# Strassen weight sums in another order: rounding of weights ahead of a batch's squares, GpSimd's staged sums regrouped, one chunk's last sums on VectorE

## The chip, the cores and the metric

The kernel runs on one core of a Trainium2 chip. The time is device microseconds of one execution; three executions of the kernel before gave 928.67, 924.08 and 924.61 us, median 924.61 us. A core has TensorE (PE, matrix products), VectorE (DVE), ScalarE (ACT), GpSimd (POOL) and SyncE (SP, which only issues DMAs here). Each engine works through its own list of instructions in order.

## The reference

Two blocks follow one another. Attention without a softmax: for each of 8 batches and 8 heads, with 576 positions and 64 channels, in float32,

```
kv  = einsum('bhsd,bhse->bhde', k, v)
out = einsum('bhsd,bhde->bhse', q, kv)
x   = out / sqrt(mean(out*out, axis=-1) + 1e-6) * g_norm     # then as (4608, 512)
h   = x @ w_in                    # (4608, 512) @ (512, 2048)
y   = maximum(0.01*h, h) @ w_out  # (4608, 2048) @ (2048, 512)
```

The two weight matrices arrive as float64 and have to be rounded to float32 on the chip; `x`, `h` and `y` are float32.

## The kernel before, in words

The 4608 rows of `x` are nine blocks of 512. The 2048 columns of `h` are four *chunks* `c` of 2 x 256 columns each. A product of two 2x2 block matrices is done in Strassen's way, with seven products in place of eight; the order of the seven is `ORDER = (1, 2, 6, 5, 7, 3, 4)`. Each needs sums of blocks of its sides, and those sums are what VectorE and GpSimd spend much of their time on.

**First block** (`first_block`, L1121; about 40 to 115 us). Block 0 of `x` meets chunks 0 to 2 without Strassen, while the weights are still coming. Step n of 12 does the product `h_ps` (n), a leaky ReLU on ScalarE (L1139), and the product `o_acc` of step n-1. In between, `between(n, half)` (L1168) works through the table `plan` (L1160): a number is a weight tile ("job") whose rounding is started with `round_w`, `f` finishes all roundings begun, `t` is a step of batch 0's attention tail, `a` one of the 14 steps of batch 1's attention (7 and 8 are its squares and copies out of PSUM, L415 and L421; 9 to 14 its division by the root mean square), `x` the four VectorE sums of block 1's Strassen sides. A rounding is two ScalarE instructions (L264 `add`, L262 `cut`), one on VectorE (L266), one on ScalarE (L271) and two on VectorE (L281, L284). Everything here but the sums of `x` keeps its written order on each engine. Starting a rounding also issues loads of later tiles: seven raw places (three in `stage`, four in `pairs`) hold jobs 0 to 23, then the two halves of `early` and the first third of `stage` serve jobs 24 on. Job 21 is the `w_in` tile of step 11; jobs 19, 17 those of steps 10, 9; jobs 22 and 23 are `w_out` tiles of steps 10 and 11; jobs 24 to 27 belong to chunk 3's `w_out` and are not needed for another hundred microseconds.

**Block 1 and the rest of block 0** (`rounds`, L1233; about 115 to 235 us). Now one-level Strassen runs on block 1 with chunks 0 to 3 and then on block 0 with chunk 3. Each chunk is seven *slots* t; the number of a slot over all chunks is `at = 7 * now + t`. A slot does one of the seven `h` products and, from slot 9 on, one of the seven `o` products of the chunk before. GpSimd makes, in this written order and with no freedom to reorder: `sides_w1(c)` (L702: sums of `w_in` for products 5 and 6, into the first quarter of `pairs`), its second part `more` (products 7 and 3, second quarter), `sides_w2` sums (L738), the `gs` sums of the activations (L916), and `combine(c, part)` (L780). GpSimd's first instruction of this stage (L1193) is a copy of one element that waits for the last of block 1's `x` sums.

`combine` prepares what comes after: from block 2 on the `h` products use Strassen twice, and the second-level sums of `w_in` are the same for all blocks, so they are made once, staged in `stage`, and written by SP to `w1_dram`. Part 0 uses products 5 and 6's sides, part 1 those of 7 and 3, part 2 the weights themselves (products 1, 2 together, then 4 alone). Parts 0 and 1 are four sums of 128x256 each; part 2 is four of 128x256 and four of 128x128. A sum's place in `stage` is the next third in the cycle 1, 2, 0. `put_off` hands the DMA to SP some slots later.

**Blocks 2 to 8** (about 235 to 925 us). Two-level Strassen; `read` (L814) brings the seven-fold weights from `w1_dram` into a ring of five places laid over the first-level weights. `sides_x(i)` makes `x`'s sums, its `inner` (L861) the second-level ones on GpSimd into `stage`.

Of the kernel before, what the change touches and what calls it, by code (L numbers as in the profile page):

```python
# [24 lines left out]
def kernel(  # L25
# [36 lines left out]
    nc = tc.nc  # L62
    B, H, S, D = q.shape
    DM, DF = w_in.shape
    P = 128
# [41 lines left out]
    NW = U * NE * P  # L107
# [589 lines left out]
    def add(eng, out_, a, b_, minus=False, pinned=False):  # L697
        ins = eng.tensor_tensor(out_, a, b_, op=ALU.subtract if minus else ALU.add)  # L698
        if pinned or steady or in_block_1:
            pin(ins)  # L700
# [74 lines left out]
    NG = 7 * P  # L775
    SLOT = {1: 0, 2: 1, 4: 2, 5: 3, 6: 4, 7: 5, 3: 6}
    w1_dram = [dram.tile([P, 7, 7, P], F32, name=f"w1_{c}") for c in range(NC)]
    stage_homes = itertools.cycle([view(stage, i * NW, NW) for i in (1, 2, 0)])

    def combine(c, part):  # L780


        direct = w1_sb[0][c].rearrange("p u (t r) m -> p u r t m", t=2)
        last = w1_sb[1][c][:, :, 2:, :].unsqueeze(3)
        parts = [((5, 6), pair(0, U, 2, 2, P))], [((7, 3), pair(1, U, 2, 2, P))], \
            [((1, 2), direct), ((4,), last)]

        for js, y in parts[part]:
            t = view(next(stage_homes), 0, 4, len(js), P)
            s1, s2, s3, s4 = (t[:, i, :, :] for i in range(4))  # L790
            y11, y12, y21, y22 = (y[:, u, r, :, :] for u in range(2) for r in range(2))

            add(nc.gpsimd, s1, y21, y22)
            add(nc.gpsimd, s2, s1, y11, True)
            add(nc.gpsimd, s3, y11, y21, True)
            add(nc.gpsimd, s4, y12, s2, True)
            to = w1_dram[c][:, :, AT[js[0]]:AT[js[0]] + len(js), :]
            if js[0] == 1:
                for r in range(2):
                    put_off(to[:, r, :, :], y[:, 0, r, :, :], 2 - part // 2)  # L800
            else:
                put_off(to[:, :2, :, :], y[:, 0, :, :, :], 2 - part // 2)
            put_off(to[:, 2, :, :], y22, 2 - part // 2)
            put_off(to[:, 3:, :, :], t, 2 - part // 2)


    reads = [(c, k) for _ in range(2, NB) for c in range(NC) for k in ORDER]
# [313 lines left out]
    def first_block(between):  # L1121
# [27 lines left out]
        for t in range(4):  # L1149
# [10 lines left out]
    plan = {(1, 0): (5, f, t), (1, 1): (t, 6, f, t), (2, 0): (t, 7, f, t), (2, 1): (8, f, t, t),  # L1160
            (3, 0): (9, f, t, a), (3, 1): (10, f), (4, 0): (11, f, a), (4, 1): (12, f),
            (5, 0): (13, f, a), (5, 1): (14, f), (6, 0): (15, f), (6, 1): (16, f),
            (7, 0): (a, a, 17, f), (7, 1): (a, 18, f), (8, 0): (a, 19, 24, f),
            (8, 1): (a, 20, 25, f), (9, 0): (a, a, 21, f), (9, 1): (a, 22, a, f),
            (10, 0): (a, 23, f, a), (10, 1): (x,), (11, 0): (26, f)}
    loaded, x_sides = 12, None

    def between(n, half):  # L1168
        nonlocal loaded, x_sides
        for what in plan.get((n, half), ()):  # L1170
            if what == f:
                finish_w()
            elif what == x:
                x_sides, _, sums, _ = sides_x(1)
                go(sums)
            elif what in (t, a):
                go(tail if what == t else a_steps, 1)
            else:
                round_w(what)
                to = what + 7 if what < 17 else {22: 28, 23: 28, 26: 28}.get(what, 25)  # L1180
                while loaded <= min(to, 31):
                    load_w(loaded)
                    loaded += 1
                    if loaded in (13, 16):
                        load_pair(1, {13: 2, 16: 3}[loaded], homes=homes_1[{13: 2, 16: 3}[loaded]])
# [8 lines left out]
    h_sides, more = sides_w1(0)  # L1194
    more()
    sides_w2(0)[1](0)
    for part in range(2):
        combine(0, part)
    sides_w2(0)[1](1)
    in_loop = True  # L1200

    LATE_ONE = {15: 2, 16: 2, 17: 1, 18: 1, 19: 2}
    A_SLOTS = {18: 1, 19: 2, 22: 1, 23: 1, 24: 2, 25: 1, 26: 1, 27: 2, 28: 1, 29: 1, 30: 1, 31: 1,
               34: 2}
    DIRECT = {23: 0, 25: 1, 27: 2, 29: 3}
    READS = {28: 2, 30: 4, 32: RING}
    PARTS = {33: ("11", "12"), 35: ("22",), 37: ("21",)}

    FINE_SLOTS = {1: 1, 2: 1, 4: 1, 9: 1, 10: 2, 11: 1, 12: 1, 15: 1, 16: 2, 17: 2, 18: 1, 19: 1,
# [24 lines left out]
    for i, chunks in rounds:  # L1234
# [7 lines left out]
        for c in chunks:  # L1242
            now += 1
            nxt = units[now + 1] if now + 1 < len(units) else (NB, 0)
            g_sides = {}
            h_steps = product_h(now, h_sides, x_sides, g_sides) if one else \
                product_h_two(i, c, now, quarters, g_sides, second_of(now - 2))
            for t in range(7):
                slot = 7 * c + t
                go(h_steps, 1)  # L1250
                if not one:

                    if t == 6:
                        go(h_steps, 1)
                    if slot in LATE_SLOTS:
                        go(late, 1)
                    for _ in range(FINE_SLOTS.get(slot, 0)):
                        go(a_steps, 1)
                    if i + 1 < NB:
                        if slot == 20:  # L1260
                            x_sides, new_quarters, sums, inner = sides_x(i + 1)
                        if slot in (20, 21, 22):
                            go(sums, 2 if slot == 20 else 1)
                        if slot == 24:
                            inner(0)
                        elif slot == 25:
                            inner(1)
                    load_some()

                if now - 1 in seconds:  # L1270
                    for half in range(2):
                        if t == (6 if half else 4):
                            inner_g(now - 1, half)
                    if t == 5 and now - 1 < 2 * NC + NC - K:
                        inner_w2(units[now - 1][1])
                if (7 * now + t == 7 * NC + 4):
                    while writes:
                        pin(nc.sync.dma_start(*writes.pop()))
                if slot in HELD and i == NB - 1:
                    pass  # L1280
                elif waited == LAG:
                    go_o()
                elif o_queue:
                    waited += 1
                write_later()
                at = 7 * now + t
                for key in PARTS.get(at, ()):
                    if at == 33:
                        part_os = os
                    load_part(part_os, key)  # L1290
                if at in READS:
                    read(READS[at])
                if one:
                    if at in DIRECT:
                        combine(DIRECT[at], 2)
                    if t == 3 and nxt[0] < 2 and nxt[1] != c:
                        h_sides, more_h = sides_w1(nxt[1])
                        combine(nxt[1], 0)
                    if t == 5 and nxt[0] < 2 and nxt[1] != c:
                        more_h()  # L1300
                    if t == 0 and units[now - 1][1] != c and now > 0:
                        combine(c, 1)
                    if not rest and rounded < len(w_jobs):
                        steps = rounding(rounded)
                        rest.extend((3, 3, 1))
                        rounded += 1
                    if rest:
                        go(steps, rest.popleft())
                    if loaded < min(rounded + 2, len(w_jobs)):
                        load_w(loaded)  # L1310
                        loaded += 1
                    if at in (15, 16):
                        load_pair(2, at - 15)
                    go(late, LATE_ONE.get(at, 0))
                    go(a_steps, A_SLOTS.get(at, 0))
                    load_some(2 if at in (19, 20) else 1)
                    if at == 7 * NC - 4:
                        x_sides, _, sums, _ = sides_x(0)
                    elif at == 7 * N1 - 4:
                        x_sides, new_quarters, sums, inner = sides_x(2)  # L1320
                    if at in (7 * NC - 4, 7 * NC - 3, 7 * N1 - 4, 7 * N1 - 3):
                        go(sums, 2)
                    if at == 7 * N1 - 3:
                        inner(0)
                    elif at == 7 * N1 - 2:
                        inner(1)

            for _ in range(2 if i == NB - 1 and c == NC - 1 else 0):
                go(h_steps, 1)
                go_o()  # L1330
            go(h_steps)
            if c == NC - 1 and i != 1 and i + 1 < NB:
                inner(2)
                quarters = new_quarters
            by_two = NC + NC - K <= now < len(units) - 2
            if by_two:
                seconds[now] = (os, store(i))
            o_queue.append(product_o(now, g_sides, os, store(i), by_two))
# [32 lines left out]
```

## Time and profile before

| what | us |
|---|---|
| median of three executions | 924.61 |
| the profiled execution, its own time | 926.94 |
| its span, first to last instruction | 925.1 |
| TensorE busy in it (matmul) | 909.7 |
| GpSimd busy | 392.9 |
| VectorE busy | 610.7 |
| ScalarE busy | 347.6 |

The profiled execution was 2.33 us above the median, and 1.84 us of its time lie outside its span. "Busy" of TensorE counts a product that runs at half clock like any other. Where a row has `[4.78 <-POOL pairs L698]` the engine stood idle 4.78 us ahead of it, until an instruction of GpSimd that writes `pairs` was done. L698 is the helper `add`, so nearly all sums of VectorE and GpSimd carry that line and are told apart by the tiles they name.

### The profile page before, as it was taken

How to read it: one execution, taken by the hardware profiler on the slowest of the kernel's cores; microseconds unless marked ns; L12 is line 12 of the kernel's file. 1: busy time of each engine (PE TensorE's matmuls, PEld its weight loads, DVE VectorE, ACT ScalarE, POOL GpSimd, SP SyncE). 2: the span in 40 equal slices, each digit the busy share in tenths (PEclk: the TensorE clock that was granted, in tenths of full speed). 3: DMA queues.
4: the chain of work that ended last, by engine and by line, in shares of the span. 5: the costliest groups of instructions: out<-in, count | busy, mean ns of one | idle time of the engine just before them, and what ended most of it. 6: DMA issues, size and time to landing. Idle time of an engine off the chain costs nothing.

```text
span 925.1 us, 18145 instructions
## 1 busy us (share of the span) xinstructions
PE 909.7 (98%) x7024; PEld 786.1 (85%) x7024; DVE 610.7 (66%) x1119; ACT 347.6 (38%) x679; POOL 392.9 (42%) x475
## 2 busy tenths in 40 slices
PE   8999979999999999999999999999999999999998
PEld 4444468888898999999999999999999999999997
DVE  5764863556556877577856785687658755755565
ACT  5756543222334332433243324333343333223330
POOL 2000099988642374216422642264225522543322
PEclk9999999999999999999999999999999999999999
DMA  9997264897999678867897788757765676667632
GB/s 262 244 243 200 68 226 153 256 279 226 287 310 309 218 224 250 260 218 219 246 268 231 223 232 263 236 165 219 241 179 181 187 220 200 183 188 221 199 116 92
DMA packets 92405, 202.16 MB, mean 219 GB/s; under 512 B 10016, under 2 KB 44448, under 8 KB 92320
## 3 DMA queue, kind: packets, MB, share of 16 engines
q1 hardware_dynamic: 81344, 189.14, 69.0%
q10 hardware_dynamic: 10528, 10.69, 3.4%
q8 instruction: 56, 0.92, 0.4%
q0 software_dynamic: 448, 1.18, 0.3%
q14 instruction: 29, 0.24, 0.1%
HBM read 173.44 MB, written 27.53 MB: 217 GB/s over the span
## 4 chain that ended last, share of the span: by engine, by line
PE 84%; DMA 9%; POOL 2%; DVE 2%; issue 1%; ACT 1%; SPq 0%; POOLq 0%; ACTq 0%; DVEq 0%
PE o_c L126 19%; PE o_a L126 18%; PE h_ha L126 11%; PE h_hb L126 10%; PE h_hc L126 8%; PE h_hd L126 8%; DMA stage<-in_moe_w_in_dram 3%; PE o_ps L126 2%; DMA pairs<-in_moe_w_in_dram 2%; DMA q_in<-in_q_dram 2%; PE h_b L126 2%; PE h_a L126 2%; POOL pairs L698 1%; PE h_c L126 1%; POOL stage L698 1%
## 5 line engine op out<-in xcount | busy, mean ns | idle before, releaser
L698 POOL TENSOR_TENSOR gs<-g 128x512 f32<-128x512 f32 x66 | 84.0, 1272 | 249.5 <-ACT g L909 249.5
L909 ACT ACTIVATE g<-g 128x512 f32<-128x512 f32 x127 | 80.1, 631 | 142.5 <-DVE g L698 142.5
L1028 ACT COPY w_all<-h_ha 128x512 f32<-128x512 f32 x84 | 49.0, 583 | 171.0 <-PE h_ha L126 165.3
L126 PE MATMUL o_c<-pairs,gs 128*128 128x256 f32 x392 | 93.2, 381 | 0.0
L126 PE MATMUL o_a<-pairs,gs 128*128 128x256 f32 x392 | 93.0, 380 | 0.0
L698 DVE TENSOR_TENSOR o<-h_hb,o 128x128 f32<-128x128 f32 x104 | 29.9, 287 | 83.2 <-ACT pairs L1028 83.1
L698 DVE TENSOR_TENSOR o<-o_a,o 128x512 f32<-128x512 f32 (+1 forms) x93 | 62.7, 674 | 30.4 <-PE o_a L126 30.1
L126 PEld LDWEIGHTS o_c<-pairs,gs 128*128 128x128 f32 x392 | 71.3, 190 | 9.4 <-POOL pairs L698 1.2
L126 PEld LDWEIGHTS o_a<-pairs,gs 128*128 128x128 f32 x392 | 71.3, 190 | 8.1
L698 DVE TENSOR_TENSOR o<-o_c,o 128x512 f32<-128x512 f32 x80 | 54.8, 686 | 31.8 <-PE o_c L126 31.7
L126 PE MATMUL h_ha<-stage,w_all 128*128 128x128 f32 x448 | 59.9, 276 | 1.4 <-POOL stage L698 1.4
L126 PEld LDWEIGHTS h_ha<-stage,w_all 128*128 128x128 f32 x448 | 56.7, 192 | 4.6 <-POOL stage L698 1.6
L698 DVE TENSOR_TENSOR g<-g,pairs 128x512 f32<-128x512 f32 x84 | 55.7, 689 | 1.9
L698 POOL TENSOR_TENSOR pairs<-g 128x128 f32<-128x128 f32 x52 | 23.8, 457 | 75.7 <-PE h_hb L126 47.4
L698 DVE TENSOR_TENSOR w_all<-h_hc,w_all 128x512 f32<-128x512 f32 x56 | 38.4, 685 | 15.8 <-PE h_hc L126 15.5
L698 DVE TENSOR_TENSOR o<-h_hd,o 128x128 f32<-128x128 f32 x78 | 22.2, 284 | 38.2 <-ACT pairs L1028 38.0
L126 PE MATMUL h_ps<-xT,w_all 128*128 128x512 f32 (+1 forms) x104 | 45.0, 580 | 2.0 <-DVE w_all L284 2.0
L126 PE MATMUL h_hb<-stage,w_all 128*128 128x128 f32 x336 | 46.7, 275 | 0.0
L1193 POOL COPY pairs<-xt 1x1 f32<-1x1 f32 x1 | 0.2, 177 | 108.0 <-PE o_acc L126 108.0
L1028 ACT COPY pairs<-h_hb 128x384 f32<-128x384 f32 x84 | 40.1, 477 | 13.8 <-PE h_hb L126 12.9
L698 POOL TENSOR_TENSOR gs<-g,gs 128x512 f32<-128x512 f32 x33 | 45.2, 1369 | 0.0
L698 POOL TENSOR_TENSOR gs<-gs,g 128x512 f32<-128x512 f32 x33 | 44.1, 1335 | 2.6
(237 smaller groups left out, 2280.5 us busy)
## 6 DMA issues: line engine op xcount, KB each, us to landing
w_all<-w SPq DMA_DIRECT2D x196, 448.0 KB, 4.1
pairs<-w SPq DMA_DIRECT2D x56, 512.0 KB, 4.3
out_dram<-o ACTq DMA_DIRECT2D x35, 256.0 KB, 5.1
v_in<-in_v_dram SPq DMA_DIRECT2D x27, 288.0 KB, 4.7
k_in<-in_k_dram SPq DMA_DIRECT2D x26, 288.0 KB, 4.4
q_in<-in_q_dram SPq DMA_DIRECT2D x52, 144.0 KB, 5.6
q_in<-in_q_dram SPq DMA_DIRECT2D x52, 140.0 KB, 5.5
w<-stage SPq DMA_DIRECT2D x12, 512.0 KB, 4.2
```

Source lines behind the costliest of these rows:

```text
L126: pin(nc.tensor.matmul(*args, **kw))
L698: ins = eng.tensor_tensor(out_, a, b_, op=ALU.subtract if minus else ALU.add)
L909: first_turn(nc.scalar.activation(t, t if src is None else src, func=AF.Prelu, alpha=SLOPE))
L1028: nc.scalar.copy(q[:, at], bank)
L1193: pin(nc.gpsimd.tensor_copy(pair(0, NW)[:1, :1], x_sides[4][:1, 0, :1]))
```

## The change

Three things change; the work computed is the same.

1. `plan`: jobs 19 to 25 are rounded in the order of their numbers, where before it was 19, 24, 20, 25, 21, 22, 23, and 19 to 22 one at a time with `f` after each. Jobs 20 and 21 stand between attention steps 7 and 8, job 23 ahead of steps 9 and 10. Which loads a rounding triggers follows: job 26's load goes with job 21, 27's with 24, 28's with 25.
2. GpSimd's order: `combine` becomes a generator with a pause after each two sums. Ahead of the loop only `combine(0, 0)` is made; `combine(0, 1)` follows `sides_w1(1)` in slot 3; `combine(c, 0)` and `combine(c, 1)` for c from 1 to 3 stand together in slot t = 0 of chunk c. `combine(0, 2)` moves from GpSimd in slot 23 to VectorE in slots 15, 16, 18 and 19, two sums each. The last parts of chunks 1, 2, 3 move from slots 25, 27, 29 to 24, 26, 28.
3. `HOMES` names each staged sum's place in `stage`, in units of 512 columns; the sources that exist already are handed to SP a slot or two sooner, and reads from `w1_dram` begin in slot 22 in place of 28 and end their first five in slot 30 in place of 32.

```diff
-    stage_homes = itertools.cycle([view(stage, i * NW, NW) for i in (1, 2, 0)])
-    def combine(c, part):
+    HOMES = {(0, 0): (2,), (0, 1): (4,), (1, 0): (0,), (1, 1): (2,), (2, 0): (4,), (2, 1): (0,),
+             (3, 0): (4,), (3, 1): (0,), (0, 2): (2, 4), (1, 2): (2, 4), (2, 2): (0, 2), (3, 2): (4, 3)}
+    def combine(c, part, eng=None):
+        eng = eng or nc.gpsimd
...
-        for js, y in parts[part]:
-            t = view(next(stage_homes), 0, 4, len(js), P)
+        for home, (js, y) in zip(HOMES[c, part], parts[part]):
+            t = view(stage, home * NW // 2, 4, len(js), P)
...
-            add(nc.gpsimd, s1, y21, y22)
-            add(nc.gpsimd, s2, s1, y11, True)
-            add(nc.gpsimd, s3, y11, y21, True)
-            add(nc.gpsimd, s4, y12, s2, True)
+            add(eng, s1, y21, y22)
+            add(eng, s2, s1, y11, True)
+            yield
+            add(eng, s3, y11, y21, True)
+            add(eng, s4, y12, s2, True)
...
-                    put_off(to[:, r, :, :], y[:, 0, r, :, :], 2 - part // 2)
+                    put_off(to[:, r, :, :], y[:, 0, r, :, :], 1)
             else:
-                put_off(to[:, :2, :, :], y[:, 0, :, :, :], 2 - part // 2)
-            put_off(to[:, 2, :, :], y22, 2 - part // 2)
+                put_off(to[:, :2, :, :], y[:, 0, :, :, :], part // 2)
+            put_off(to[:, 2, :, :], y22, part // 2)
             put_off(to[:, 3:, :, :], t, 2 - part // 2)
+            yield
...
-            (7, 0): (a, a, 17, f), (7, 1): (a, 18, f), (8, 0): (a, 19, 24, f),
-            (8, 1): (a, 20, 25, f), (9, 0): (a, a, 21, f), (9, 1): (a, 22, a, f),
-            (10, 0): (a, 23, f, a), (10, 1): (x,), (11, 0): (26, f)}
+            (7, 0): (a, a, 17, f), (7, 1): (a, 18, f), (8, 0): (19, f, a, 20, f),
+            (8, 1): (21, f, a, 22, f), (9, 0): (23, f, a, a), (9, 1): (a, 24, a, f),
+            (10, 0): (a, 25, a, f), (10, 1): (x,), (11, 0): (26, f)}
...
-                to = what + 7 if what < 17 else {22: 28, 23: 28, 26: 28}.get(what, 25)
+                to = what + 7 if what < 17 else {17: 25, 18: 25, 19: 25, 20: 25, 24: 27}.get(what, 26 if what < 24 else 28)
...
-    for part in range(2):
-        combine(0, part)
+    go(combine(0, 0))
...
-    DIRECT = {23: 0, 25: 1, 27: 2, 29: 3}
-    READS = {28: 2, 30: 4, 32: RING}
+    DIRECT = {24: 1, 26: 2, 28: 3}
+    READS = {22: 2, 28: 4, 30: RING}
...
-                        combine(DIRECT[at], 2)
+                        go(combine(DIRECT[at], 2))
+                    if at == 15:
+                        direct_0 = combine(0, 2, nc.vector)
+                    if at in (15, 16, 18, 19):
+                        go(direct_0, 1)
                     if t == 3 and nxt[0] < 2 and nxt[1] != c:
                         h_sides, more_h = sides_w1(nxt[1])
-                        combine(nxt[1], 0)
+                        if now == 0:
+                            go(combine(0, 1))
...
                     if t == 0 and units[now - 1][1] != c and now > 0:
-                        combine(c, 1)
+                        for part in range(2):
+                            go(combine(c, part))
```

## The prediction

> **What bounds the kernel now.** The page's busy times come first: TensorE is busy 909.7 of 925.1 us, so only the 15 us in which it isn't, and stretches at a lower clock, can be won. The waits of TensorE (line, releaser: total, times, longest) name four that the change touches:
>
> ```profile
> PE 909.7 (98%) x7024; PEld 786.1 (85%) x7024; DVE 610.7 (66%) x1119; ACT 347.6 (38%) x679; POOL 392.9 (42%) x475
> ...
> PE h_b L126 <- POOL pairs L698: 4.8, 1, 4.8
> PE h_ps L126 <- DVE w_all L284: 2.0, 1, 2.0
> ...
> PE h_ha L126 <- POOL stage L698: 1.4, 1, 1.4
> PE h_c L126 <- DVE g L698: 1.2, 1, 1.2
> ```
>
> By the timeline they end at 102.83 (h_ps, step 11, waits for job 21's rounding), 121.52 (h_c), 136.93 (h_b: product 6 of chunk 1 waits for its sum) and 244.23 us (h_ha). The busy times by stretch show what an idle stretch costs beside itself (window: length, PE, PEld, DVE, ACT, POOL busy with counts, granted clock, DMA share, GB/s):
>
> ```profile
> 104.00:106.00 2.00, 2.00 (x4) 0.73 (x3) 0.93 (x2) 2.00 (x6) 0.00 (x0) 0.56 0.07 14
> 132.00:134.00 2.00, 0.15 (x1) 0.00 (x0) 1.30 (x2) 0.63 (x1) 2.00 (x3) 1.00 0.70 234
> 136.00:138.00 2.00, 1.07 (x3) 0.90 (x4) 0.00 (x0) 0.00 (x0) 1.84 (x3) 0.50 0.97 262
> 142.00:144.00 2.00, 2.00 (x11) 1.75 (x10) 0.00 (x0) 0.92 (x2) 1.92 (x3) 1.00 1.03 254
> ```
>
> After the waits of 2.0 and 4.8 us the clock was 0.5; after those of 1.2 and 1.4 us it stayed 1.0. GpSimd's timeline (start, length) shows why h_b waits: four staged sums, combine(0, 1), stand ahead of what product 6 needs.
>
> ```profile
> 127.14 0.72 POOL L698 TENSOR_TENSOR stage<-pairs 128x256 f32<-128x256 f32 x1
> 127.94 1.06 POOL L698 TENSOR_TENSOR stage<-stage,pairs 128x256 f32<-128x256 f32 x1
> 128.97 1.23 POOL L698 TENSOR_TENSOR stage<-pairs 128x256 f32<-128x256 f32 x1
> 130.17 0.72 POOL L698 TENSOR_TENSOR stage<-pairs,stage 128x256 f32<-128x256 f32 x1
> ...
> 133.50 1.71 POOL L698 TENSOR_TENSOR pairs<-w_all 128x512 f32<-128x512 f32 x1
> 135.28 1.59 POOL L698 TENSOR_TENSOR pairs<-pairs,w_all 128x512 f32<-128x512 f32 x1
> ```
>
> GpSimd runs without a gap from 114.4 to 202.8 us. The chain of waits shows the last stall: a write of `stage` released by an unrelated output write, then GpSimd, then TensorE.
>
> ```profile
> 235.75 2.21 DMA out_dram<-o
> ...
> 238.02 2.31 DMA w<-stage
> ...
> 240.46 1.43 POOL stage L698 x2
> ```
>
> [...] The trace halves from about 104.2 to 107.6 and 134.9 to 141.6 us[...]. [...] VectorE's L284 took 0.69 us at 109.9, 1.65 at 116.6 under GpSimd. [...]
>
> **Part 1, the roundings.** Cost of one alone, from rows between 84 and 110 us: ScalarE 0.57 (L264), 0.67 (L262 to its end), VectorE 0.42, ScalarE 0.54, then VectorE 0.73 + 0.61; back to back 2.47 per job. Before, ScalarE idles 2.46 us at 88.09 for job 24's load, and job 21 comes behind steps 9 and 10. Laid out in the new order from 82.0 us (squares and copies 1.90 per step, steps 9 and 10 2.42 on VectorE): job 19's ScalarE work ends at 84.3, the squares of step 7 at 86.2, 20 at 88.4, 21 at 90.9 (VectorE 92.4), step 8 at 92.8, 22 at 95.1, ReLU 9 at 95.6, 23 at 97.8 (VectorE 99.3), steps 9 and 10 at 101.8, 24's first half, spread and second half at 105.5, ReLU 10 at 106.1.
>
> So w_in of step 11 is ready at 92.4 instead of 102.78 and that wait goes. But its gain goes with it. `o_ps` of step 8 waits 0.4 us for later copies; `h_ps` 11 ends at 104.5; ReLU 10, at 104.91 before, is now 106.1: TensorE waits 1.6 us there, and 0.7 for ReLU 11 at 110.2. It reaches block 1 at about 113.7 (before 114.93). VectorE has steps 13 and 14 done at 110.7, job 25's last two at 112.1, and four `x` sums by 0.61: 114.5, against 114.2. GpSimd starts on those, so at 114.5 to 114.8 (before 114.43), and its first sum for product 6 is ready 3.25 later, at 117.9: TensorE waits again. h_c then waits for VectorE, which before took 7.3 us from its last `x` sum to `g` (job 26, copies of `o`, job 27's cut[...]): 121.9 against 121.52. I value part 1 at -0.3 us (a loss). It is a loss of 3 if each single rounding takes 0.5 us more than laid out, a gain of 1.1 if the `x` sums slip ahead of job 25's last two. Loads: 27 and 28 are issued 6 and 9 us later, behind jobs 24 and 25; they land by 113 (4 to 7 us, from the DMA table) and are read at 117.4 and 124.0, so they are hidden; if late they delay only ScalarE's and VectorE's order there.
>
> **Part 2, GpSimd's order.** Without combine(0, 1) the sums of chunk 1's product 6 are ready 3.72 us (127.14 to 130.86) earlier after GpSimd's start: 22.44 - 3.72 = 18.7 after it. TensorE arrives 10.6 us after h_c, at 132.5; GpSimd is ready at 133.3. The wait falls from 4.78 to about 0.8, and with a wait below 1.4 the clock should stay full. Half clock cost h_b 3.57 from start to start, not 1.73, and o_a 2.38: 1.84 + 0.65 = 2.5 us. So part 2 gains 3.7 + 2.5 = 6.2. What is late next: combine(0, 1) now precedes `more`, and overwriting the second quarter of `pairs` waits for SP's write of it, which stands behind the `sides_w2` write and job 30's four loads; I put 0.2 us on TensorE (0 to 1). The activations' sums end 29.6 after the start, not 33.1, and from there to slot 21 GpSimd leads TensorE by at least 5 us (chunk 2's product 6: 37.9 against 43.7; chunk 3's: 59.5 against 69.4). The pairs of combines moved to t = 0 cost 5.7 each, inside that lead; without it, one to one.
>
> combine(0, 2) on VectorE is 4 x 0.42 + 4 x 0.29 = 2.8 us[...]; VectorE was busy 5.4 to 5.7 of each 10 us there, and a bank of PSUM is wanted again 5.2 us after a product, so some 4 us of delay are covered. Its second half goes to place 4, which combine(2, 0) fills last: GpSimd ends that 51.5 after its start (166), the 512 KB write takes 4.2, so place 4 is free at about 170.8; VectorE gets there at 169.4. A wait of 1.4 us holds up the adds behind it, and is covered. TensorE: 0.
>
> **Part 3, places, writes, reads.** GpSimd loses 4.6 us of work and ends the last combine near 217 instead of 228.3; its write then stands two slots ahead of block 1's output writes. The h_ha wait, 1.44, should go (0 if the write is released by an output write again). The read in slot 22 waits for combine(0, 2)'s write some 3 us; q, k, v loads and sources' writes are queued behind it on SP, with at least 10 us until they are read. The copies to `w1_dram` are the same bytes. Cost 0; from 250 us on TensorE is never idle, so every gain reaches the end.
>
> **Sum.** -0.3 + 6.2 - 0.2 + 1.4 = 7.1 us. The profiled execution's 926.94 (span 925.1 and 1.84 around it) becomes 919.8; it lay 2.33 above the median, so the median becomes 917.5. [...]
>
> **Rivals.**
> - *The halving stays* (0.17). TensorE's several short waits between 104 and 122, or the 0.8 left at h_b, suffice to halve the clock, or part 1's chain slips 3 us and GpSimd with it. For: 1.98 sufficed, and I leave 2.1 at h_c. Against: 1.24 and 1.44 didn't. Worth 2.5 to 4: 920 to 922, within 0.5% of before.
> - *The gain of part 1 is real* (0.13). If the `x` sums come 2 us or more earlier, GpSimd, h_c and h_b all shift: 913 to 915. For: ScalarE's 2.46 us for job 24's load go. Against: single roundings need about 0.5 us more each than pairs, which eats them.
> - *VectorE waits for a place in `stage`* (0.10, the slower side). VectorE works in order; with combine(0, 2) it hangs on SP's write of place 4, and SP stands in line for q, k, v loads. What is queued behind: adds that free PSUM banks, and batch 2's transposes. Up to 4 us is free, beyond it each us is one of TensorE. It ends above 924.6 once the write lands 4 + 7 = 11 us after VectorE asks, past 180 us, and slower by 0.5% (929) past 185. For: one SP write waited 10.2 us for an output write. Against: none of those outputs is in flight before 225 us.
>
> The forecast itself has 0.60: 915 to 920.
>
> **How the numbers follow.** A measurement of this kernel tells about 0.5%, 4.6 us, from no change: faster means below 920.0, slower above 929.2. Faster: 0.58 of the forecast's 0.60, and 0.13, and a little of the first rival, 0.73. Slower: 0.07 of the last. Same: 0.20. The range takes in part 1's bounds and both nearer rivals: 912.5 to 923.
>
> **What would show it.** Right: h_b's wait below 1.5 us with the clock at 1.0 between 133 and 142; no wait for `w_all` L284; GpSimd's L1193 at 114 to 115; h_ha's wait gone. Wrong: L1193 past 117 (part 1's working), a clock of 0.5 past 130, VectorE waiting for a `w<-stage` write over 4 us, or new waits of TensorE between 140 and 240.

## The result and the profile after

Over 20 executions of each kernel the time went from 925.74 us (median; 923.76 to 929.28) to 922.03 us (920.8 to 926.31): a ratio of 0.9963, with an interval of 0.9950 to 0.9977, so 3.4 us of gain (2.1 to 4.6); the two medians differ by 3.7. The forecast was 7.1 us. The sign is right, and the interval excludes a ratio of 1; the size is half of what was forecast. The median lies inside the range of 912.5 to 923, but not in the 915 to 920 to which the forecast itself gave 0.60, and by the prediction's own bound of 0.5% it counts as no change. The 20 executions after lie in two groups, ten at 920.8 to 921.5 us and ten at 922.6 to 926.3, and the median falls into the gap between them.

The profiled execution after took 921.17 us, its span is 919.5. It shows nearly every step of the forecast. First the page's busy times of the kernel after:

```profile
PE 907.0 (99%) x7024; PEld 784.0 (85%) x7024; DVE 620.3 (67%) x1127; ACT 347.1 (38%) x679; POOL 390.5 (42%) x467
```

Then its waits of TensorE (line, releaser: total, times, longest):

```profile
PE o_acc L126 <- ACT g L1143: 1.9, 2, 1.4
PE h_c L126 <- DVE g L698: 1.8, 1, 1.8
...
PE o_c L126 <- POOL pairs L698: 1.1, 1, 1.1
PE h_b L126 <- POOL pairs L698: 1.0, 1, 1.0
PE o_a L126 <- POOL gs L698: 0.8, 1, 0.8
```

The waits for `w_all` (2.0) and at `h_ha` (1.4) are gone, and `h_b`'s has fallen from 4.8 to 1.0. TensorE now waits for ScalarE's ReLU at `o_acc`, as part 1 of the forecast had it. The line `o_c <- POOL pairs` is new and was not foreseen; that at `o_a` was, with 0.2 us. The busy times by stretch (columns as before) show the clock:

```profile
104.00:106.00 2.00, 0.56 (x2) 0.14 (x2) 0.64 (x1) 2.00 (x5) 0.00 (x0) 1.00 0.81 248
132.00:134.00 2.00, 1.09 (x5) 0.99 (x6) 1.30 (x2) 0.67 (x2) 1.92 (x3) 1.00 0.81 186
136.00:138.00 2.00, 2.00 (x11) 1.74 (x11) 0.27 (x1) 2.00 (x5) 1.92 (x2) 1.00 0.10 33
142.00:144.00 2.00, 1.41 (x7) 1.26 (x8) 1.14 (x2) 0.63 (x1) 2.00 (x2) 1.00 1.00 344
```

The clock is 1.00 in all four stretches; before, two of them stood at 0.56 and 0.50. TensorE's busy time is 2.7 us less (909.7 to 907.0) for the same 7024 products, none of them at half clock. GpSimd's timeline (start, length) around product 6 of chunk 1 (L1197 is what was L1193 before):

```profile
114.17 0.18 POOL L1197 COPY pairs<-xt 1x1 f32<-1x1 f32 x1 [107.76 <-DVE xt L698]
...
129.79 1.73 POOL L698 TENSOR_TENSOR pairs<-w_all 128x512 f32<-128x512 f32 x1
131.59 1.26 POOL L698 TENSOR_TENSOR pairs<-pairs,w_all 128x512 f32<-128x512 f32 x1
132.81 0.91 POOL L698 TENSOR_TENSOR stage<-pairs 128x256 f32<-128x256 f32 x1
```

GpSimd starts at 114.17. The sums for product 6 end at 132.85, 18.7 us after the start, which is the forecast's number to the tenth. `combine(0, 1)` begins only then. In the chain of waits, the write of `stage` that held up `h_ha` is no longer at the end. Another one stands some 30 us earlier:

```profile
207.59 5.64 DMA w<-stage
216.42 4.44 POOL gs L698 x3
222.33 3.76 POOL stage L698 x4
229.04 1.99 PE o_c L126 x8
```

This is the new wait. In slot 28, `combine(3, 2)` (the eight `stage` sums that end at 227.8) now stands ahead of the two sums for `o_c`, which start at 227.73 and 228.96, and TensorE stands 1.14 us for the first of the two: it goes on at 229.04, when that one is done. The forecast had the last `combine` end near 217 us. GpSimd would have been there sooner, had it not stood for 5.20 us up to 192.37 us. GpSimd's timeline there, and then the part of SP's (DMA issues) in front of it:

```profile
185.88 1.29 POOL L698 TENSOR_TENSOR gs<-g,gs 128x512 f32<-128x512 f32 x1
192.37 0.73 POOL L698 TENSOR_TENSOR stage<-pairs 128x256 f32<-128x256 f32 x1 [5.20 <-issue]
```

```profile
176.29 0.44 SPq L735 DMA_DIRECT2D w<-stage  x1
...
184.15 1.87 SPq L138 DMA_DIRECT2D k_in<-in_k_dram  x1
186.06 0.43 SPq L138 DMA_DIRECT2D v_in<-in_v_dram  x1
186.59 0.38 SPq L735 DMA_DIRECT2D w<-pairs  x1
187.02 1.66 SPq L735 DMA_DIRECT2D w<-w_all  x2
188.72 1.08 SPq L735 DMA_DIRECT2D w<-stage  x1
```

The sum at 192.37 is the first of `combine(3, 0)`, whose place is 4. VectorE had filled place 4 with the second half of `combine(0, 2)` by 178.2. The code hands its write to SP a slot later, and SP issues it only at 188.72, behind the loads of k, v and q; `combine(3, 0)` begins 3.65 us after that. I read the stand as one for place 4; the page itself puts it down to "issue". The run `places` below tests it.

### The profile page after: what moved, and what is told of

It reads as the page before. It is cut to its first block, busy times and chain, and to the rows that moved or that the text cites. A ratio compares the mean times of both kernels' runs of the same rounds, so it can differ in the third digit from the quotient of the medians.

```text
span 919.5 us, 18154 instructions
## 1 busy us (share of the span) xinstructions
PE 907.0 (99%) x7024; PEld 784.0 (85%) x7024; DVE 620.3 (67%) x1127; ACT 347.1 (38%) x679; POOL 390.5 (42%) x467
## 4 chain that ended last, share of the span: by engine, by line
PE 80%; DMA 10%; POOL 4%; DVE 2%; ACT 2%; issue 1%; SPq 0%; POOLq 0%; ACTq 0%; DVEq 0%
PE o_c L126 19%; PE o_a L126 18%; PE h_ha L126 11%; PE h_hb L126 10%; PE h_hc L126 8%; PE h_hd L126 8%; DMA stage<-in_moe_w_in_dram 3%; PE o_ps L126 3%; DMA q_in<-in_q_dram 2%; DMA stage<-in_moe_w_out_dram 2%; POOL pairs L698 1%; DMA pairs<-in_moe_w_in_dram 1%; POOL stage L698 1%; PE h_b L126 1%; POOL gs L698 1%
## 5 line engine op out<-in xcount | busy, mean ns | idle before, releaser
L1197 POOL COPY pairs<-xt 1x1 f32<-1x1 f32 x1 | 0.2, 177 | 107.8 <-DVE xt L698 107.8
L126 PE MATMUL o_acc<-w,g 128*128 128x512 f32 x96 | 43.8, 599 | 1.9 <-ACT g L1143 1.9
```

What stands on the lines that cost most here:

```text
L126: pin(nc.tensor.matmul(*args, **kw))
L1197: pin(nc.gpsimd.tensor_copy(pair(0, NW)[:1, :1], x_sides[4][:1, 0, :1]))
```

## The experiments

The kernels ran in three groups, each on one chip together with the kernel before: `b_again`, `plan_only`, `rest_only` and `warm`; `after_again`, `rest_again`, `warm5` and `late32`; `c01_only`, `places`, `rest_places` and `gps02`. All ratios are against the kernel before of the same group, and microseconds are the ratio's distance from 1, times its median there. Between the groups only ratios are compared.

### Is the kernel before steady? (b_again)

The kernel before, unchanged.

> The kernel before, unchanged, as a second sample with the granted clock of every execution. The forecast's theory (the profiled execution is typical but for about 2 us): most executions have a mean clock near 0.994[...], and ratio 1.000. Rival: the profiled execution was halved in more windows than most; then the mean clock of the faster half is 0.996 to 0.998, and the time follows the clock, about 1.7 us for 0.002.

Ratio 0.9998 (0.9984 to 1.0013), 926.66 us. Most executions have a mean clock of 0.996 (8 of 14), some 0.998 (4), and few the 0.994 (2) of the execution that the prediction was built on: the rival of the expectation came. No execution of the kernel before in the three groups has more than 0.998. In this profile the wait at `h_ps` is only 0.79 us and the clock behind it is 1.00 (100 to 132 us); behind that at `h_b` (4.78 us) it is 0.50. Its busy times by stretch:

```profile
134.00:136.00 2.00, 0.00 (x0) 0.00 (x0) 0.97 (x1) 0.56 (x1) 1.92 (x2) 0.78 0.98 302
136.00:138.00 2.00, 1.86 (x4) 1.52 (x5) 0.00 (x0) 0.00 (x0) 1.84 (x4) 0.50 0.98 247
138.00:140.00 2.00, 2.00 (x6) 1.63 (x5) 0.00 (x0) 0.04 (x1) 2.00 (x3) 0.50 0.26 88
140.00:142.00 2.00, 2.00 (x6) 1.56 (x6) 0.00 (x0) 0.55 (x1) 2.00 (x3) 0.51 1.00 305
```

So the idle wait of 4.78 us and the half clock behind it are in both profiles of the kernel before. The halving at 104 us was seen in one execution, in which the `h_ps` wait was long.

### Part 1 alone, and all but part 1 (plan_only, rest_only, rest_again)

`plan_only` is before with the new plan and its loads; `rest_only` and `rest_again` are after with the old plan.

```diff
-            (7, 0): (a, a, 17, f), (7, 1): (a, 18, f), (8, 0): (19, f, a, 20, f),
+            (7, 0): (a, a, 17, f), (7, 1): (a, 18, f), (8, 0): (a, 19, 24, f),
...
-                to = what + 7 if what < 17 else {17: 25, 18: 25, 19: 25, 20: 25, 24: 27}.get(what, 26 if what < 24 else 28)
+                to = what + 7 if what < 17 else {22: 28, 23: 28, 26: 28}.get(what, 25)
```

> The kernel before with part 1 alone (the new table and its loads). My working: TensorE's wait for job 21 goes, but VectorE's x sums end where they did, so GpSimd's L1193 stays at 114 to 115 us and h_b still waits 4 to 5 us and is followed by half clock: 0 to -1 us. Rival (part 1 carries a good share of the gain): -2 to -3.5 us.

> The changed kernel with the old table of the first block (parts 2 and 3 alone). If the gain is GpSimd's order, -3 to -3.5 us against before, as the whole change; h_b waits below 1.5 us. Rival (the parts only help together, because a first half clock between 104 and 108 us comes back): -1.5 us or less.

> The changed kernel with the old table, again, beside the changed kernel. If the old table's start of GpSimd follows the load of job 24 (113.65 to 117.01 us in three profiles, with that wait at 1.3, 2.5 and 3.3 us), its times spread by 4 us or more where the changed kernel's spread less, with the fastest below the changed kernel's fastest. Median 0 to -3 us against the changed kernel.

`plan_only`: 1.0006 (0.9993 to 1.0019), with `h_b` still waiting 4.79 us. `rest_only`: 0.9932 (0.9906 to 0.9958), -6.3 us, about twice the 3 to 3.5 that were expected. `rest_again`, in the second group: 0.9953 (0.9937 to 0.9970), -4.4 us; the kernel after itself, beside it (as `after_again`), 0.9965 (0.9952 to 0.9978). Part 1 is thus not what gains.

What it does is best seen in when GpSimd starts. Under the old plan that hangs on the load of job 24, for which ScalarE stands in order. ScalarE's wait for that load, and GpSimd's start, in `rest_only`:

```profile
90.69 0.68 ACT L264 ACTIVATE add<-early 128x512 uint32<-128x512 uint32 x1 [3.27 <-DMA early<-in_moe_w_out_dram]
...
117.01 0.18 POOL L1197 COPY pairs<-xt 1x1 f32<-1x1 f32 x1 [110.61 <-PE o_acc L126]
```

All profiles with the old plan, in us; the last column counts from the start of TensorE's first `h_ps` product, which itself lies between 22.6 and 23.8 us:

| old plan | ScalarE's wait for job 24 | GpSimd's start | after the first `h_ps` |
|---|---|---|---|
| `warm5` | none | 111.99 | 89.07 |
| `c01_only` | 0.36 | 112.17 | 89.51 |
| `rest_places` | 0.79 | 112.88 | 89.92 |
| `warm` | 0.98 | 113.76 | 90.18 |
| `b_again` | 1.29 | 113.65 | 90.39 |
| `rest_again` | 2.42 | 114.32 | 91.52 |
| before | 2.46 | 114.43 | 91.58 |
| `rest_only` | 3.27 | 117.01 | 93.48 |

The new plan takes this wait out and puts a fixed one in its place: 1.4 to 1.5 plus 0.4 us at `o_acc`, in every profile of it. GpSimd's start, counted in the same way, is 91.54 to 91.62 in five of its six profiles (after, `places`, `gps02`, `plan_only`, `late32`) and 93.87 in the sixth (`after_again`). The old plan's middle is 90.3. The execution that the prediction was built on was one with a late load, and so gave no sign of these 1.2 us. The expectation of `rest_again` had one miss: the old plan's times spread less (920.39 to 924.05) than those of the kernel after (920.85 to 926.02), and not more.

> The changed kernel, unchanged, on the same chip as its relatives. If the parts add up (part 1 0, the rest about -6 us): ratio 0.993 to 0.994. If the first measurement holds (part 1 costs 3 us as soon as GpSimd's order is better): 0.996 to 0.997, and the old table (below) 2 to 3 us faster in the same runs. GpSimd's L1197 stands 91.5 us after the first h_ps in each profile of the new table (in both so far, 91.54 and 91.59).

The kernel after again, unchanged: its executions lie in two groups, eight at 920.9 to 921.3 us and thirteen at 922.7 to 926.0. The profiled one, 923.45 us, is of the second group. Two lines of its timeline, ScalarE's and GpSimd's, and below them ScalarE's wait for the same load in the first profile of the kernel after:

```profile
75.17 0.68 ACT L264 ACTIVATE add<-stage 128x512 uint32<-128x512 uint32 x1 [4.48 <-DMA stage<-in_moe_w_out_dram]
...
116.71 0.18 POOL L1197 COPY pairs<-xt 1x1 f32<-1x1 f32 x1 [110.28 <-DVE xt L698]
```

```profile
69.22 0.68 ACT L264 ACTIVATE add<-stage 128x512 uint32<-128x512 uint32 x1 [0.23 <-DMA stage<-in_moe_w_out_dram]
```

The tile was waited for 4.48 us, ahead of anything that the change touches, and GpSimd's start is 2.3 us later, counted from the first `h_ps`, where the expectation had the same 91.5 us in every profile. But the 0.23 us of the first profile need not be the usual value: the profile before has 3.62 us there (at 72.83). Some executions of the second group also have a mean clock of 0.998 (5 of the 13 here, 4 of the 10 in the first result). So what makes the second group is open; a late tile and a mean clock of 0.998 were each seen in it.

### What the half clock is worth (warm, warm5)

Products whose result nobody reads, issued by TensorE ahead of product 6 of chunk 1, inside its wait; eleven of them in `warm`, five in `warm5`.

```diff
+                if 7 * now + t == 9:
+                    warm_ps = ps_m.tile([P, NT], F32, tag="oa", name="warm_ps")
+                    for _ in range(5):
+                        matmul(warm_ps, lhsT=w2_sb[0][0][:, 0, :P], rhs=w2_sb[0][0][:, 0, :],
+                               start=True, stop=True)
```

> The kernel before with eleven products of 128x512 that nobody reads, put ahead of chunk 1's product 6, 4.7 us of TensorE work in the place of the 4.8 us of waiting. If the half clock after that wait costs 2.5 us in the usual execution, as in the forecast: -2.5 us. If the usual execution loses less to it: -0.5 to -1.5. If the filler is later than GpSimd's sum: 0 or slower.

> The kernel before with five unread products in place of eleven: one of them is 0.86 us and not 0.43 (the first filler took 9.4 us), so these are 4.3 us inside the wait of 4.8. If the half clock after the wait costs 2.5 us and reaches the end: -2.5 us, ratio 0.997. If TensorE only meets the next wait sooner (the first product on stage sums at 244 us, held by a write that waits for an output write): -0.5 to +1.

`warm` was mis-sized: one product of this shape takes 0.86 us, eleven take 9.4, and the 4.78 us wait was overrun by 4.6. It came to 1.0055 (1.0031 to 1.0078) and tells little. `warm5` puts 4.45 us into the wait: 0.9989 (0.9975 to 1.0003), -1.0 us. Its busy times by stretch:

```profile
134.00:136.00 2.00, 1.50 (x7) 1.35 (x8) 0.00 (x0) 0.00 (x0) 1.84 (x3) 1.00 0.92 231
136.00:138.00 2.00, 2.00 (x11) 1.77 (x10) 0.00 (x0) 0.59 (x1) 2.00 (x4) 1.00 0.40 139
138.00:140.00 2.00, 2.00 (x12) 1.74 (x10) 0.00 (x0) 1.74 (x4) 2.00 (x3) 1.00 0.82 249
```

The clock stays full at `h_b`, and from the start of `h_b` to `o_ps` (fourteen products on) TensorE takes 24.4 us, where `b_again` took 27.2 and before 26.8. In the stage the half clock therefore costs 2.4 to 2.9 us, as the forecast's 2.5. It is not fixed: in `plan_only`, where the clock stood at half for 3.4 us behind the same wait and not for 6.8, the stretch takes 26.05 us, 1.7 more. But of the 22 executions of `warm5` half have a mean clock below 1.0 again, and those take 924.8 to 930.5 against 921.8 to 925.0. Where it is lower in those isn't shown. The wait at `h_ha`, which `warm5` keeps, is my guess, and the profile doesn't bear it out: it has this wait at 1.48 us, with a clock of 1.00 from 230 to 250 us.

### The last part in slot 28 (late32)

The kernel after with chunk 3's last part back in slot 29, behind the two `sides_w2` sums.

```diff
-    DIRECT = {24: 1, 26: 2, 28: 3}
+    DIRECT = {24: 1, 26: 2, 29: 3}
```

> The changed kernel with the last part of chunk 3 back in slot 29, behind the sums of w_out that product 7 of the last first-level chunk waits for at 229 us. If that new wait of 1.1 us comes from the order of those two: the wait is gone and -1.1 us against the changed kernel. Rival: GpSimd is late there anyhow, because it idled 5.2 us at 187 us for a place in stage, and the wait moves to the first stage product at 238 us: 0.

0.9994 (0.9978 to 1.0009): 925.59 us against 923.37 for the kernel after beside it, slower by about 2 us, where the expectation had 1.1 less or no difference. The wait at `o_c` is gone, and a longer one takes its place. GpSimd's timeline and TensorE's:

```profile
240.39 0.72 POOL L698 TENSOR_TENSOR stage<-xt,stage 128x256 f32<-128x256 f32 x1 [5.67 <-DMA w<-stage]
...
241.17 1.65 PE L126 MATMUL h_ha<-stage,w_all 128*128 128x128 f32 x6 [2.66 <-POOL stage L698]
```

The stretch behind it, in the busy times:

```profile
242.00:244.00 2.00, 2.00 (x10) 1.80 (x9) 0.00 (x0) 0.58 (x1) 2.00 (x4) 0.50 1.03 330
```

The write of that part is not done when block 2's sums want its place. So the earlier slot costs 1.14 us at `o_c` and saves more: 2.66 at `h_ha`, and the half clock after it (0.50 from 242 to 244 us).

### One move alone (c01_only)

The kernel before with `combine(0, 1)` in slot 3 and `combine(1, 0)` beside `combine(1, 1)`, and nothing else. The sources of `combine(0, 1)` then go out in slot 6, one slot after `more` has overwritten them: that part of `w1_dram` holds chunk 1's values, and the result is wrong. Sums, bytes and products are as many as before, so it serves to time the order of the sums, and for nothing else. Here one sees what the kernel after's earlier hand-over of the sources is for.

```diff
-    for part in range(2):
-        combine(0, part)
+    combine(0, 0)
...
-                        combine(nxt[1], 0)
+                        combine(nxt[1], 0) if now else combine(0, 1)
...
+                        if c == 1:
+                            combine(c, 0)
                         combine(c, 1)
```

> The kernel before with one move alone: combine(0, 1) from ahead of the loop to slot 3, and combine(1, 0) from slot 3 to slot t = 0 of chunk 1, beside combine(1, 1). Plan, places, reads and the last parts stay as before. Theory (the order of GpSimd's sums carries nearly the whole gain): the wait of TensorE at h_b falls from 4.8 to about 1.0, which is -3.7, and the half clock after it goes, about -1: 921 to 922 us, ratio about 0.995, while the wait at h_ha (1.4) stays. Rival (the places, the early sources and combine(0, 2) on VectorE carry half of the gain): -2 or less, 923.5 to 925, because a new wait between 140 and 240 us eats it.

0.9949 (0.9933 to 0.9965): -4.7 us (3.2 to 6.2). The waits in TensorE's timeline:

```profile
119.26 1.99 PE L126 MATMUL h_c<-xt,pairs 128*128 128x256 f32 x8 [1.79 <-DVE g L698]
130.91 1.99 PE L126 MATMUL h_b<-xt,pairs 128*128 128x256 f32 x8 [1.02 <-POOL pairs L698]
140.59 1.99 PE L126 MATMUL o_a<-pairs,gs 128*128 128x256 f32 x8 [0.78 <-POOL gs L698]
237.03 0.94 PE L126 MATMUL h_ha<-stage,w_all 128*128 128x128 f32 x6 [1.59 <-POOL stage L698]
```

The theory held and the rival fell: this exchange of two groups of four sums gives the fall at `h_b` (4.78 to 1.02) and keeps the clock there (`h_b` takes 1.99 us in place of 3.78, and the profiled execution's mean clock is 1.000), and its ratio is no worse than that of the whole change (0.9963 and 0.9965; the intervals overlap). The wait at `h_ha` stays, and 10 of the 17 executions have a mean clock below 1.0, much as in `warm5`. It is not all that parts 2 and 3 can give: `rest_places` below, beside it on the same chip and with the same old plan, takes 3.2 us less, and the intervals do not meet.

### Three places exchanged (places, rest_places), and combine(0, 2) on GpSimd (gps02)

`places` is the kernel after with the staged sums of chunk 3 kept off place 4; `rest_places` is the same with the old plan; `gps02` is the kernel after with `combine(0, 2)` on GpSimd.

```diff
-             (3, 0): (4,), (3, 1): (0,), (0, 2): (2, 4), (1, 2): (2, 4), (2, 2): (0, 2), (3, 2): (4, 3)}
+             (3, 0): (0,), (3, 1): (2,), (0, 2): (2, 4), (1, 2): (4, 2), (2, 2): (0, 2), (3, 2): (4, 3)}
```

```diff
-                        direct_0 = combine(0, 2, nc.vector)
+                        direct_0 = combine(0, 2)
```

> The kernel after with three places of staged sums exchanged: combine(3, 0) to place 0, combine(3, 1) to place 2, and combine(1, 2) to places 4 and 2. Theory (GpSimd's stand of 5.2 us ahead of combine(3, 0), for place 4, makes the wait of 1.1 us at o_c): the stand shrinks below 1 us, GpSimd comes to the last sums of chunk 3's w_out sides some 4 us sooner, the wait at o_c goes and nothing takes its place: 1.1 us less than the kernel after, 921 to 922 us. Rival (the last sums of activations or VectorE hold GpSimd there anyway): GpSimd's stand moves behind them, the wait at o_c stays near 1 us, same time as the kernel after, 922 to 923.5 us.

> The same three places, with the old plan of roundings and loads. If the two are independent: 1 to 2 us less than parts 2 and 3 alone, which gave ratios of 0.993 and 0.995: 919.5 to 921 us, the fastest of all. If the new plan is needed to hold the rest up: no better than the kernel after with the places, 921 us or more.

> The kernel after with the eight sums of combine(0, 2) on GpSimd in slots 15, 16, 18 and 19, in place of VectorE. If GpSimd leads by 5 us or more there, as the prediction has it, then 4.6 us more of its work are covered at first, and what counts is the last part: it comes to the sums for o_c at 229 us later, less what it no longer stands waiting for place 4, so the wait of 1.1 us there becomes 1 to 3: 0 to 2 us more than the kernel after, 922 to 925 us. If the lead is smaller than thought, a new wait at an h product of chunk 2 or 3 (160 to 200 us) of up to 4 us: 925 to 927 us.

`places`: 0.9958 (0.9939 to 0.9976), 922.09 us. The profile shows what was meant: GpSimd has no gap ahead of `combine(3, 0)`, the two sums for `o_c` start at 224.31 and 225.54 in place of 227.73 and 228.96, and TensorE does not wait there. GpSimd keeps 3.4 of the 5.2 us: behind the exchange it stands 1.42 and 0.95 us for other writes of `stage`. The span is 918.3 against 919.5. As a gain in time this is not shown: by the ratios (0.9958, and 0.9963 and 0.9965 for the kernel after in the other groups) it is about 0.5 us, inside the intervals.

`rest_places`: 0.9915 (0.9898 to 0.9932), 919.14 us (917.34 to 921.02, six executions): -7.9 us, and the fastest kernel of the study, below both given ones. Against `places`, beside it on the same chip, only the plan differs, and the intervals do not meet. TensorE's waits near the end of the first block, `places` first:

```profile
106.18 3.70 PE L126 MATMUL o_acc<-w,g 128*128 128x512 f32 x8 [1.45 <-ACT g L1143]
110.31 3.70 PE L126 MATMUL o_acc<-w,g 128*128 128x512 f32 x8 [0.44 <-ACT g L1143]
```

```profile
101.27 3.70 PE L126 MATMUL h_ps<-xT,w_all 128*128 128x512 f32 x8 [0.31 <-DVE w_all L284]
109.19 3.67 PE L126 MATMUL o_acc<-w,g 128*128 128x512 f32 x8 [0.46 <-DVE w L284]
```

1.89 us under the new plan, 0.77 under the old, when job 24's load is nearly on time. In all three pairs that differ in the plan alone, the new plan has the larger median: `plan_only` against `b_again` by 1.2 us (0.4 against all 33 executions of before in that group), after against `rest_again` by 1.2, `places` against `rest_places` by 2.9. Only the last is outside the intervals.

`gps02`: 0.9945 (0.9929 to 0.9962), 921.55 us; no slower than the kernel after (0.9963 and 0.9965, in other groups), where the expectation had 0 to 2 us more. GpSimd is done with the activations' sums at 191.1 us instead of 187.2, then stands 2.21 us for the place in `stage` instead of 5.20 (the page names the write of `stage` as what ended it), and the wait at `o_c` is 1.17 instead of 1.14. Most of the work that the change took off GpSimd came back as standing: moving it gained nothing on TensorE's path.

What it can cost was seen once. In the profiled execution of `rest_again`, VectorE's timeline, then TensorE's:

```profile
174.43 1.05 DVE L698 TENSOR_TENSOR stage<-w_all 128x128 f32<-128x128 f32 x1 [3.98 <-DMA w<-stage]
...
185.40 1.97 PE L126 MATMUL o_c<-pairs,g 128*128 128x256 f32 x8 [2.18 <-DVE o L698]
```

VectorE stood 3.98 us for place 4, its adds of `o` came late, and TensorE waited 2.18 us for one. This is the third rival's mechanism, at its mild end.

## Why the prediction was right, and where it was wrong

- **Part 1's -0.3: the first term that failed, by its size.** The layout was right in its places. Foreseen: the `w_all` wait gone, waits of 1.6 and 0.7 at the ReLUs, GpSimd's start at 114.5 to 114.8, `h_c` at 121.9. Found: gone, 1.44 and 0.43, 114.17, 121.26. But the worth was reckoned against one execution, whose load of job 24 was 2.46 us late. Counted from the first `h_ps`, GpSimd started 91.58 us after it there, against a middle of 90.3 for the old plan and 91.5 to 91.6 for the new one: a loss of about 1.2 us and not of 0.3. The medians of the three pairs put it at 1.2, 1.2 and 2.9 us. TensorE's waits are 1.9 us under the new plan always, 0.5 to 3.2 under the old.
- **Part 2, the wait at `h_b`: right.** 18.7 us after the start, foreseen and found; the wait 1.02 for 0.8.
- **Part 2, the half clock: right in the stage.** 2.5 us foreseen, 2.4 and 2.9 found from `h_b` to `o_ps` (1.7 in `plan_only`). But without that stretch 11 of the 22 executions of `warm5` still have a mean clock of 0.996 or 0.998, where isn't shown; with them it comes to only 1.0 us by the ratio.
- **"I put 0.2 us on TensorE (0 to 1)": low.** `o_a` waits 0.78 us for the activations' sums, in every kernel with the move.
- **`combine(0, 2)` on VectorE, "TensorE: 0": right in after's profile,** with longer sums and a longer stand for place 4 than thought. A sum of 128x256 took 1.17 to 1.53 us, where VectorE's of this shape had 0.42 before (425 ns, `o<-o_a,o`), all eight 7.8 in place of 2.8; the stand was 3.30 us at 173.58 in place of 1.4. In one execution of `rest_again` 3.98 was too much.
- **Part 3, "Cost 0": the second term that failed.** The wait at `h_ha` went, as foreseen (-1.44). But the prediction had the last `combine` end near 217 us, ahead of all that TensorE wants. It ended at 227.8, in front of sums that TensorE wanted at 227.9. Of these 10.8 us, 3.4 go with the stand for place 4 (in `places` it ends at 224.4). For the others the traces show stands for other places (1.42 and 0.95 us in `places`) and longer sums (up to 1.44 and 1.98 us in place of 0.73 and 1.27), but no full account. I had followed place 4 up to VectorE's own use of it and not to the next one, `combine(3, 0)`, though I had named the SP queue that held up the write. Cost: 1.14 us. From 260 to 900 us TensorE is busy 639.86 of 640 us before and after alike, so it reaches the end, as the gains do.
- **From one execution to the median: the step that carried the first error on.** The forecast for the profiled execution was 919.8; it came to 921.17, 1.4 us more: the 1.14 at `o_c` and 0.6 more at `o_a`, less some tenths at the start. The prediction took off the same 2.33 us from the profiled execution after as from the one before. But the one before lay 1.20 us above the median of 20 (926.94, 925.74), and the one after 0.86 below (921.17, 922.03). Together 1.37 + 2.06 = 3.4 us, which is the distance between 7.1 and the 3.7 us that the medians differ by. The 1.20 is of the size of the late start, 91.58 against 90.3. The clock was a second sign: 0.994, with 3.4 us (104.3 to 107.7) and 6.8 us (134.9 to 141.7) at half clock (10.2 x 0.5 of 925 us is 0.0055), where most executions have 0.996 or 0.998. The 0.86 comes from the two groups of the kernel after: the profiled execution was one of the faster group, which was luck.
- **What is accounted for.** Of the 3.4 us, part 1 has about 0.9 (1.2 for 0.3), `o_a` 0.6 and `o_c` 1.1. The last 0.8 us stay open.
- **The signs.** All four that the prediction named for being right were seen, and one of those for being wrong as well: new waits of TensorE between 140 and 240 us, 0.78 at `o_a` and 1.14 at `o_c`.
- **The rivals.** The first one's number, 920 to 922, is nearly what was measured, but its mechanism is not: no half clock is in after's profile, and 4 of its 20 executions have a mean clock of 0.998. The second one's gain of part 1 came out as a loss. The third one's wait of VectorE for a place came, and cost 2.18 us in one execution of a variant.

## What to carry to other kernels

Before a wait is valued, look at what its length depends on. A wait behind a load varies from run to run (ScalarE's for job 24: none to 3.27 us), and a new order that replaces it by a fixed wait has to be held against its usual length, not against the one profile at hand. When buffer places are set by hand, follow each place to its next writer and that writer's place in the order; the exchange of three places here brought GpSimd's last sums 3.4 us forward without any other work moving. And where several edits come together, take them one by one: the exchange of two groups of four sums alone is timed at 4.7 us, by its ratio no less than the whole change; the earlier hand-over is what makes it usable; and the new plan of roundings took a part of the gain back.

## What was not expected of the hardware

- The length of a short idle of TensorE doesn't by itself tell whether half clock follows. After waits of 1.98 us (before, 102.83) and 2.66 us (`late32`, 241.17) the clock was 0.50 (104.4 to 107.6, and 242 to 244 us). Around waits of 1.92 us (`rest_again`, 102.72) and 2.42 us (`rest_only`, 105.42) it was 1.00 from 100 to 120 us. The wait of 2.18 us (`rest_again`, 185.40) lies in an execution whose mean clock is 1.000; a half clock of 3.4 us, as in before from 104.3 to 107.7, would be 0.0018 of it. What decides is not shown.
- A write's issue was the long part (after). Place 4's sums were done by 178.2 us, the write, handed to SP a slot later, was issued at 188.72, and the sums that wanted the place started 3.65 us after that.
- A float32 product of 128x512 was two instructions in the trace: five of them were ten, and took 4.45 us (`warm5`). I had sized `warm` by one instruction each.
